# One LayerNorm group for token tiles 0 and 1, GpSimd multiplies ordered behind VectorE's, and a new list of the first tasks

## The chip, the cores and the metric

The kernel runs on one core of one Trainium2 chip. The metric is the device time of one execution in microseconds (us), the median of several runs. A core has five engines that run side by side, each through its own list of instructions in order: TensorE (PE in the profile; its weight loads, which overlap its matmuls, are PEld), VectorE (DVE), ScalarE (ACT), GpSimd (POOL), and SyncE (SP), which here issues nearly all transfers (DMAs). They wait for each other by semaphores.

## What is computed

The reference is one transformer block with a linear attention, for 2048 tokens of width 512 (32 heads of 16) and a gated feed-forward part of width 1376. A vector `c` gives six rows of modulation.

```
mod = silu(c) @ w_mod                    # sa, ca, ga, sb, cb, gb, 512 each
h   = layernorm(x) * (1 + ca) + sa
q, k, v = h @ wqkv, per head
pq, pk  = q @ w_phi, k @ w_phi           # per head, 16 x 16
phi_q   = [softmax(pq), softmax(-pq)]    # phi_k alike from pk
kv = phi_k^T v ;  z = sum of phi_k over the tokens
o  = (phi_q kv) / (phi_q z + 1e-6)
x  = x + ga * (o @ wo)
h  = layernorm(x) * (1 + cb) + sb
x  = x + gb * ((sigmoid(h @ w_gate) * (h @ w_up)) @ w_down)
```

Weights, inputs and the output are bf16.

## The kernel before

The tokens are cut into 16 tiles of 128. Everything is a task: a name, the engines that it may run on with the planner's costs, what it reads and writes, and the buffers that it uses (class `Graph`, L109). The program's order is the string `ORDER` (L39): every task's name once, in one list, with `@A`, `@D` or `@P` where it doesn't run on its first engine. `arrange` (L137) hands out the buffers in this order, `emit` (L270) issues the tasks in this order, and each engine runs its own in the order of the list. So the list is the schedule: a task that isn't ready holds up whatever stands behind it on its engine. There are eight PSUM banks, seven 2 KB buffers for features (`r2k`), eight `xn` buffers and so on (`CAPS`, L250).

The stages, by task names (the number is the token tile unless said):

- Start: `ld_...` are SP's loads (of x, wk, wv, pieces `wm` of w_mod, and so on); `warm` are matmuls on zeros that fill TensorE's time (`warm0` is six, `warm1_0` to `warm1_11` one each); `c1`, `c2`, `c3` make silu(c). `tpw`, `wTc`, `fold`, `foldc` fold w_phi into the key weights, and with `wqT` (a transposing load) into the query weights. `modc1.0` and `modc1.1` with their copies `modc1c0`, `modc1c1` make sa and ca; `modca` makes ga, `modc2` the other three rows.
- First LayerNorm (L695 to L760), in groups `LG` of tiles: `st1` the statistics (VectorE, two instructions), `rs1` the reciprocal root of a group, `nmr1` minus mean times root (one small instruction a tile), `xn1` the normalized tile, then for each of four column blocks `tph` (TensorE transposes it) and `hm1` (scale and shift into `h1T`). Two groups (`TD`) are transposed by DMA (`xT1`) instead.
- Keys and values: `K` and `V` are four matmuls of 512 columns each (in two halves `a`, `b` for the first tiles); `e` the two exponentials (ScalarE, L776), `n` the sums over features (VectorE, L780), `r` their reciprocals (VectorE or ScalarE), `phi` the products (L787, GpSimd or VectorE), `va` the copy of the values (L836), `kv` the accumulation into two banks. `kvz`, `kvn` mask the sums into `kvb` (L294, L299).
- Queries: `Q`, `qe`, `qn`, and `qphi` in two halves (L784), then `pT`, a transpose by DMA.
- From there, tile by tile: `num` (phi_q times kv), `rd`, `u` (division), `tpo`/`oT`, `out` (times wo), `x1`, the second LayerNorm (`st2`, `rs2`, `nmr2`, `xn2`, `xnT`, `mod`), and in chunks of 1, 1, 2, 4, 4 and 4 tiles the feed-forward part: `g`, `u` with a dot in its name, `tg` (tanh), `hm`, `y`, `fin`, `st`. `tsw` switches ScalarE's table to tanh. `wo` and `wd` multiply ga and gb into the weights (GpSimd, L851 and L860); gb and ga go through DRAM (`gw`, `gr`) to be spread over the partitions. `ld_wd2` loads the last piece of w_down, into the tile that the `warm` matmuls read, so it waits for the last of them.

Of the kernel before, what the change touches and what calls it, by code (L numbers as in the profile page):

```python
# [39 lines left out]
bd wdz warm0 c1 warm1_0 warm1_1 warm1_2 warm1_3 warm1_4 warm1_5 ld_x0b ld_x0a ld_wk0 tpw1 tpw0 warm1_6 warm1_7 c2 mask4 st1_3 st1_2 st1_1 ld_x1b rs1_2 rs1_1  # L40
nmr1_2 ld_wk1 xn1_3@A c3 wTc1 ld_x1a pmem tpw2 wTc0 nmr1_1 st1_6 wTc2 ld_wm00b st1_0 tpw3 xn1_1 tph13 tph10 xn1_2 tph22 tph20 tph21 wTc3 fold10 rs1_0@P fold12
st1_7 foldc10 ld_wm00a foldc12 fold11 modc1.0 rs1_4@P ld_x2b warm1_8 warm1_9 foldc11 modc1c0 st1_5 tph11 tph12 warm1_10 ld_wm01b warm1_11 st1_4 rs1_3@P
hm1_20@A xn1_0 nmr1_4 hm1_10 hm1_11@A hm1_21@A tph01 tph23 fold13 tph00 xn1_6 xn1_7 ld_wm01a st1_11 hm1_01@A foldc13 st1_10 modc1.1 K3a modc1c1@D ld_x2a
hm1_00@A tph02 nmr1_3 hm1_23 rs1_6@P hm1_13@A hm1_02 st1_9 st1_8 xn1_5 tph03 K0a tph41 hm1_03@A K2a tph40 xn1_4 hm1_22@A hm1_12@A hm1_41@A hm1_40 wqT1 nmr1_6
ld_x3a st1_15 fold01 K2b foldc01 tph42 hm1_42@A K0b K3b e0.0 ld_wv0 tph32 tph30 tph31 wqT3 tph33 rs1_5@P nmr1_5 K1a hm1_32 xn1_11 hm1_30@A st1_14 n0.0 st1_12
xn1_10 e2.0 xn1_9 K1b e3.0 rs1_8@P V3a V3b va3 V0a wqT2 xn1_8 V2a hm1_31@A V2b tph43 nmr1_8 xn1_15 xn1_14 ld_wmga wqT0 V0b fold03 V1a modca.0 modca.1 hm1_33
tph50 e1.0 n2.0 V1b K5a r0.0@A modcac hm1_50 n3.0 hm1_43@A foldc03 xT1_11 fold02 tph52 fold00 foldc02 phi0.0 va2 foldc00 xT1_10 va1 n1.0 va0 K5b K4a r3.0
# [8 lines left out]
qn6.0 wo0 wo3 kv15.0 kvz0 kvn0 kv13.4 kv14.4 kv15.4 kvz1 kvn1 num0a num1a num2a wo2 rd0a wo_all rd1a qe3.0 u0a num0b num4a num1b rd0b Q11 qe5.0 rd2a u0b u2a
rd4a num2b qn3.0 u1a rd1b tpo0 Q8 qphi6.0@P qphi6.1@P oT0 out0 num4b rd2b u1b wd0 qe11.0 u2b qphi3.1@P qphi3.0@P x1_0 rd4b st2_0 qe8.0 Q7 qe7.0 tpo1 oT1 Q10
Q9 out1 Q15 oT2 rs2_0 qn5.0 nmr2_0 xn2_0 u4a u4b x1_1 qn7.0 tsw xnT0 out2 qphi5.1@P qphi5.0@P pT6 mod02 mod00 qphi7.0@P pT3 mod03@A mod01@A qe15.0 qphi7.1@P
Q13 g0.8 x1_2 tg0.8 g0.1 st2_1 wd1 rs2_1 tg0.1 u0.8 u0.1 g0.0 num3b g0.4 hm0.1 hm0.8 pT5 qe9.0 tg0.4 g0.9 wd2 u0.4 u0.9 rd3b u3b tg0.9 g0.5 num3a hm0.4 hm0.9
# [999 lines left out]
```

## Time and profile before

| | |
|---|---|
| median of 3 runs | 203.47 us (203.35 to 204.83) |
| span of the execution profiled | 202.2 us |
| TensorE busy | 194.4 us, 96% of the span |
| VectorE busy | 160.6 us, 79% |
| ScalarE busy | 105.3 us, 52% |
| GpSimd busy | 104.2 us, 52% |
| mean granted clock of TensorE | 0.998 |
| moved by DMA | 22.92 MB |

The time of a run is taken outside of the profile; the span is from the profile's first instruction to its last. A timeline row is the start in us, the length in us, the engine, the line, the operation, the output and inputs with their sizes, and how many instructions were merged into it; in brackets the idle time before it and what ended that. A group row has count, busy time, mean ns of one, and idle time before it. Neighbouring instructions of an engine overlap a little, so the time that one costs is from its start to the next one's. Matmuls are pipelined: a matmul of 512 columns is 379 ns long in the records, while the next can start well before its end.

### The profile page before, as it was taken

What the parts mean: (1) busy time and instruction counts of PE and PEld (TensorE: products, weight loads), DVE (VectorE), ACT (ScalarE), POOL (GpSimd) and SP (SyncE); (2) the same over time, 40 slices, a digit from 0 to 9 for tenths busy, and PEclk for the clock granted to TensorE, in tenths of its full rate; (3) what the DMA queues carried; (4) which work ended last, traced back from release to release, by engine and by line L of the source; (5) the groups of instructions that cost most, each with busy time, mean ns of one, the idle gap of its engine ahead of it and who ended that gap; (6) DMA issues with size and microseconds to landing.
All of it is one profiled execution on the core that took longest, in us unless ns stands there. A gap on an engine that the chain in (4) does not pass through costs nothing.

```text
span 202.2 us, 4128 instructions
## 1 busy us (share of the span) xinstructions
PE 194.4 (96%) x1447; PEld 106.2 (53%) x1471; DVE 160.6 (79%) x376; ACT 105.3 (52%) x250; POOL 104.2 (52%) x146
## 2 busy tenths in 40 slices
PE   7989999999989999999999999999999999999993
PEld 2545656455464787668844444444444444444442
DVE  3999999999999999998897796885969753326622
ACT  2899999999978975576531215212113420334100
POOL 3889978799699998867570066130030431000000
PEclk9999999999999999999999999999999999999999
DMA  5999965669963992418664243542113031000011
GB/s 169 329 262 239 289 232 111 114 71 261 396 254 77 133 109 51 82 39 108 117 79 80 53 79 85 100 104 52 26 26 81 2 78 54 28 5 26 28 54 57
DMA packets 49452, 22.92 MB, mean 113 GB/s; under 512 B 38065, under 2 KB 47634, under 8 KB 49426
## 3 DMA queue, kind: packets, MB, share of 16 engines
q1 hardware_dynamic: 48896, 22.59, 50.1%
q8 instruction: 12, 0.20, 0.4%
q14 instruction: 14, 0.11, 0.2%
q10 hardware_dynamic: 530, 0.02, 0.2%
HBM read 11.58 MB, written 2.10 MB: 68 GB/s over the span
## 4 chain that ended last, share of the span: by engine, by line
PE 70%; ACT 15%; DVE 8%; issue 2%; POOL 2%; DMA 1%; POOLq 0%; DVEq 0%
PE y_ps L485 19%; PE u_ps L447 18%; PE g_ps L447 18%; PE a_ps L356 5%; ACT h1T L751 3%; ACT e L776 3%; ACT qe L776 2%; PE num L326 2%; PE k_ps L817 2%; DVE qks L780 2%; ACT wqk_f L685 2%; PE v_ps L821 2%; DVE ks L780 1%; DMA x_sb<-in_A_x_dram 1%; DVE phi L787 1%
## 5 line engine op out<-in xcount | busy, mean ns | idle before, releaser
L457 ACT ACTIVATE tg<-g_ps 128x512 bf16<-128x512 f32 (+5 forms) x66 | 28.7, 455 | 66.8 <-PE g_ps L447 39.9
L468 DVE SCALAR_TENSOR_TENSOR wmod_sb<-tg,u_ps 128x512 bf16<-128x512 bf16 (+4 forms) x63 | 30.2, 491 | 18.0 <-ACT tg L457 11.5
L485 PE MATMUL y_ps<-wd_sb,wmod_sb 128*128 128x512 bf16 (+4 forms) x180 | 44.2, 366 | 0.2
L447 PEld LDWEIGHTS <-wg_sb 128*128 128x128 bf16 (+1 forms) x252 | 21.9, 99 | 16.1 <-issue 0.2
L447 PEld LDWEIGHTS <-wu_sb 128*128 128x128 bf16 (+1 forms) x252 | 21.7, 99 | 15.9 <-issue 0.3
L784 POOL TENSOR_TENSOR qphi<-qe,qks 128x512 bf16<-128x512 bf16 x24 | 25.1, 1064 | 4.1 <-DMA pT<-qphi 1.4
L485 PEld LDWEIGHTS <-wmod_sb 128*128 128x128 bf16 (+1 forms) x187 | 17.1, 98 | 16.0 <-issue 0.6
L447 PE MATMUL u_ps<-wT_sb,wu_sb 128*128 128x512 bf16 (+2 forms) x124 | 23.8, 322 | 0.1
L447 PE MATMUL g_ps<-wT_sb,wg_sb 128*128 128x512 bf16 (+2 forms) x122 | 23.0, 321 | 0.2
L447 PE MATMUL g_ps<-wqk_sb,wg_sb 128*128 128x128 bf16 (+4 forms) x127 | 19.9, 287 | 0.1
L447 PE MATMUL u_ps<-wqk_sb,wu_sb 128*128 128x128 bf16 (+4 forms) x127 | 19.8, 286 | 0.2
L780 DVE TENSOR_REDUCE ks<-e 128x64 f32<-128x1024 bf16 (+2 forms) x22 | 19.3, 904 | 0.2
L492 DVE TENSOR_TENSOR ot<-y_ps,x 128x512 bf16<-128x512 f32 (+2 forms) x17 | 11.1, 654 | 10.1 <-PE y_ps L485 10.1
L780 DVE TENSOR_REDUCE qks<-qe 128x64 bf16<-128x1024 bf16 x16 | 19.1, 1204 | 0.0
L376 POOL TENSOR_SCALAR ve<-mv 128x2 f32<-128x2 f32 (+1 forms) x8 | 1.8, 226 | 33.4 <-DVE mv L366 33.3
L776 ACT ACTIVATE e<-k_ps 128x512 bf16<-128x512 f32 (+2 forms) x44 | 18.3, 536 | 0.0
L776 ACT ACTIVATE qe<-q_ps 128x512 bf16<-128x512 f32 x32 | 17.1, 612 | 0.8 <-POOL phi L787 0.6
L787 POOL TENSOR_TENSOR phi<-e,kr 128x1024 bf16<-128x1024 bf16 (+2 forms) x10 | 14.9, 1501 | 2.5 <-DVE phi L787 1.2
L817 PE MATMUL k_ps<-wqk_f,h1T 128*128 128x512 bf16 x61 | 16.1, 379 | 0.1
L356 PE MATMUL a_ps<-wo_sb,oT 128*128 128x512 bf16 x60 | 15.9, 379 | 0.2
L871 PE MATMUL q_ps<-wqk_f,h1T 128*128 128x512 bf16 x61 | 15.7, 379 | 0.2
L821 PE MATMUL v_ps<-wv_sb,h1T 128*128 128x512 bf16 x61 | 15.3, 379 | 0.1
(132 smaller groups left out, 307.7 us busy)
## 6 DMA issues: line engine op xcount, KB each, us to landing
out_dram<-ot SPq DMA_DIRECT2D x15, 128.0 KB, 1.8
x_sb<-in_A_x_dram SPq DMA_DIRECT2D x6, 256.0 KB, 5.1
wmod_sb<-in_w_mod_dram SPq DMA_DIRECT2D x1, 1536.0 KB, 7.0
wu_sb<-in_B_w_up_dram SPq DMA_DIRECT2D x1, 1376.0 KB, 10.9
wg_sb<-in_B_w_gate_dram SPq DMA_DIRECT2D x1, 1376.0 KB, 10.3
wd_sb<-in_B_w_down_dram SPq DMA_DIRECT2D x1, 1280.0 KB, 7.9
wmod_sb<-in_w_mod_dram SPq DMA_DIRECT2D x4, 256.0 KB, 6.2
wqk_sb<-in_A_wqkv_dram SPq DMA_DIRECT2D x2, 256.0 KB, 4.8
```

Source lines behind the costliest of these rows:

```text
L356: pe.matmul(ap_[:], lhsT=oT[:, j, :], rhs=wo_sb[:, j, :], start=(j == 0), stop=(j == KT - 1))
L447: pe.matmul(ps[:fsz, 0:n], lhsT=w[:, j, ft * P:ft * P + fsz], rhs=h[:, j, 0:n], start=(j == 0), stop=(j == KT - 1))
L457: G.add(f"tg{k}.{ft}", {"ACT": 0.13 + n * 0.00083}, lambda e, tg=tg, g_ps=g_ps, fsz=fsz, n=n: act.activation(tg[:fsz, 0:n], g_ps[:fsz, 0:n ...
L468: dve.scalar_tensor_tensor(hm_all[:fsz, hm[k].slot, ft, 0:n], tg[:fsz, 0:n], 1.0, u_ps[:fsz, 0:n], op0=ALU.add, op1=ALU.mult)
L485: mm = pe.matmul(y[:, 0:c1 - c0], lhsT=hm_all[:fsz, hm[k].slot, ft, tl * P:(tl + 1) * P], rhs=wd_sb[:fsz, ft, c0:c1], start=(ft == 0), sto ...
L776: act.activation(ee[:, a:b, s].rearrange("p g f h -> p g (f h)"), kp[:, a * 64:b * 64].rearrange("p (g n) -> p g n", n=64), ACT.Exp, scale ...
L780: dve.tensor_reduce(ks[:, a:b].rearrange("p g s h -> p (g s) h"), ee[:, a:b].rearrange("p g s f h -> p (g s) h f"), axis=AX.X, op=ALU.add)
L784: engine(e).tensor_tensor(ph[:].rearrange("p (g s f h) -> p g s f h", s=2, f=DH, h=4)[:, :, s], ee[:, :, s], ks[:, :, 1 - s].unsqueeze(2). ...
L787: engine(e).tensor_tensor(ph[:, a * P:b * P].rearrange("p (g f h) -> p g f h", f=DH, h=4), ee[:, a:b].rearrange("p g s f h -> p (g s) f h" ...
L817: pe.matmul(kp[:], lhsT=h1T[:, j, t * P:(t + 1) * P], rhs=wqk_f[:, j, D:2 * D], start=(j == 0), stop=(j == KT - 1))
L821: pe.matmul(vp[:], lhsT=h1T[:, j, t * P:(t + 1) * P], rhs=wv_sb[:, j, :], start=(j == 0), stop=(j == KT - 1))
L871: pe.matmul(qp[:], lhsT=h1T[:, j, t * P:(t + 1) * P], rhs=wqk_f[:, j, 0:D], start=(j == 0), stop=(j == KT - 1))
```

## The change

Three things change.

The first LayerNorm's groups: tiles 0 and 1, which were groups of one, are one group; `rs1_0` now serves both, `tph0.j` transposes both tiles, `hm1_0.j` scales both. The tasks are named after the first tile of the group now (`hm1_2.1` was `hm1_21`, `hm1_10.0` was `hm1_60`). `xn1_0`, which ran on VectorE, takes the form of the others (GpSimd or ScalarE, with `nmr1_0`).

`emit` keeps the last instruction of the last VectorE task that counts as a user of the port (`phi`, `qphi`, `xn1`, `xn2`, `wo`, `wd`, some `hm1` and `mod`), and each later GpSimd task except `rs` gets a dependence on it, that is, waits for it, whether or not it uses its data.

`ORDER` is a new list as a whole. Of the rest that the diff adds (`HALF`, `QHALF`, `ROWS`, `WPQ`, `RPAIR`), all is switched off.

```diff
-LG = [[0], [1], [2, 3], [4, 5], [6, 7], [8, 9], [10, 11], [12, 13], [14, 15]]
-TD = [0, 0, 0, 0, 0, 0, 1, 1, 0]
+LG = [[0, 1], [2, 3], [4, 5], [6, 7], [8, 9], [10, 11], [12, 13], [14, 15]]
+TD = [0, 0, 0, 0, 0, 1, 1, 0]
...
+XP = list(range(16))
+PIN = 1
...
     def emit(order):
+        pinned = None
         for t in order:
...
+            body = nc.cur_bb.bb.instructions
+            n0 = len(body)
             t.fn(t.eng)
+            if PIN and t.eng in t.port and not t.name.startswith("rs"):
+                if t.eng == "DVE":
+                    pinned = body[-1].name
+                elif pinned:
+                    tc.add_manual_dep(body[n0], pinned, mybir.DependencyInfo(mybir.DependencyClass.Sync, mybir.DependencyReason.DATA), reason="port order")
```

The head of the new list, with TensorE's first keys and the first exponential:

```
bd wdz c1 warm0 pmem mask4 ld_x0a st1_1 st1_0 rs1_0 ld_x0b st1_2 nmr1_0 xn1_0 xn1_1@A c2 st1_3 rs1_2 ld_x1b st1_6 st1_7 rs1_6@P ld_wk0 tpw0 tpw1 wTc0 warm1_0
warm1_1 wTc1 ld_wk1 tpw2 tpw3 wTc3 wTc2 fold10 foldc10 fold13 foldc13 fold12 foldc12 tph0.0 fold11 foldc11 c3 nmr1_2 xn1_2 xn1_3 ld_x1a st1_5 nmr1_6 st1_4 rs1_4
ld_x2a st1_8 ld_wm00b ld_wm00a warm1_2 tph0.1 modc1.0 modc1c0@D hm1_0.0@A tph2.2 tph2.1 tph0.3 warm1_3 hm1_2.1@A tph2.3 tph2.0 xn1_7 xn1_6 warm1_4 warm1_5
warm1_6 hm1_2.0@A hm1_0.1@A ld_x2b st1_10 nmr1_4 xn1_4 xn1_5 st1_9 rs1_8@P st1_11 ld_wm01a ld_wm01b modc1.1 modc1c1 hm1_2.2 tph6.0 hm1_6.0@A tph0.2 hm1_0.2@A
hm1_0.3@A K3a K0a tph4.2 hm1_4.2@A tph4.0 K1a tph4.1 hm1_4.1@A K0b e0.0 hm1_2.3 K3b e3.0 tph6.2 tph6.3 K1b K2a e1.0 ...
```

Further on: `V4 e4.0 rs1_14 tph8.0 kv0.0 Q1 qe1.0 tph8.2 Q0 qe0.0 V3a V3b K5a va3 phi1.0@D kv1.0`; `warm1_7` stands ahead of `kv3.0`, `warm1_8` and `warm1_9` about `kv10.0`; at the end of the sums `kv15.0 kvz0 kv15.4 kvz1 kvn0 kvn1 qe7.0 Q5 qe5.0 wo0 wo1 wo_all num0a`, then `num4a Q8 warm1_10 warm1_11 ld_wd2 grb u0b tpo0 oT0`, and `xnT0 mod02@A mod01@A mod00@A mod03@A out4 Q10 ... st2_1 rs2_1 g0.2 tsw g0.9 tg0.9`. Before, that last place read `xn2_0 ... tsw xnT0 out2 ... mod02 mod00 ... mod03@A mod01@A`, and Q7 stood behind the sums.

More of the change, by code (lines that the diff above doesn't have):

```diff
@@ L39 @@
 ORDER = """
[L40 to L47, printed above, removed]
@@ L56 @@
[L56 to L59, printed above, removed]
@@ new lines @@
+nmr1_8 xn1_9 st1_13 rs1_12@P n0.0 hm1_6.2 hm1_6.3 hm1_4.0 ld_wv0 V0a wqT3 V2a wqT2 V0b tph4.3 hm1_4.3@A K2b e2.0 V2b tph6.1 va2 va0 wqT0 wqT1 fold01 fold02 V1a
+V1b va1 fold00 foldc00 xn1_8 tph8.3 xn1_11 nmr1_12 xn1_12 r0.0 phi0.0 n3.0 r3.0@A phi3.0 ld_wmga xT1_10 ld_wo xT1_11 hm1_10.3@P xn1_13 K4a K4b fold03 foldc03
+n1.0 hm1_8.3 foldc01@D hm1_6.1 st1_14 modca.0 modca.1 modcac r1.0@A foldc02 n2.0 V4 e4.0 rs1_14 tph8.0 kv0.0 Q1 qe1.0 tph8.2 Q0 qe0.0 V3a V3b K5a va3 phi1.0@D
+kv1.0 hm1_8.2@A hm1_8.0@A r2.0 nmr1_14 xn1_15 hm1_10.2@P phi2.0@D kv2.0 Q2 qe2.0 V5 tph8.1 hm1_8.1@A xn1_14@A warm1_7 kv3.0 K5b e5.0 qn1.0 qphi1.0@P qn0.0
@@ new lines @@
+phi8.0@D K15 va8 kv8.0 V14 va9 kv9.0 K12 r10.0 phi10.0 e14.0 n14.0 e13.4 n13.4 r14.0 phi14.0 r13.4 phi13.4 e13.0 n13.0 e14.4 va10 n14.4 r13.0 phi13.0 warm1_8
+kv10.0 Q6 kv11.0 warm1_9 kv11.4 kv11.2 kv11.6 e15.0 n15.0 r15.0 phi15.0 e15.4 n15.4 e12.0 n12.0 r14.4@A phi14.4@D qe6.0 r15.4@A phi15.4@D gra wo3 wo2 ld_wg0
+ld_wu0 ld_wd gwb r12.0@A phi12.0@D qn6.0 V13 va13 Q3 qe3.0 qn3.0 qphi3.0@P V12 Q7 V15 va12 kv12.0 kv13.0 kv13.4 qphi3.1 pT3 va14 kv14.4 va15 kv14.0 kv15.0 kvz0
+kv15.4 kvz1 kvn0 kvn1 qe7.0 Q5 qe5.0 wo0 wo1 wo_all num0a rd0a num1a rd1a u0a num0b rd0b num1b num4b rd4b num4a Q8 warm1_10 warm1_11 ld_wd2 grb u0b tpo0 oT0 u1a
@@ new lines @@
+u4b rd1b rd4a u1b qphi6.0@P qphi6.1@P pT6 qn5.0 qphi5.0@P u4a oT4 qphi5.1@P pT5 qe8.0 Q9 qe9.0 out0 x1_0 tpo1 oT1 num2b rd2b Q11 qe11.0 st2_0 rs2_0 wd7 qn7.0
+qphi7.1@P qphi7.0@P wd3 Q15 qe15.0 nmr2_0 num2a rd2a Q13 num3a rd3a num3b u2b u3a u2a oT2 out1 x1_1 rd3b num6a rd6a num6b rd6b u3b oT3 xn2_0 xnT0 mod02@A
+mod01@A mod00@A mod03@A out4 Q10 u6a x1_4 u6b oT6 wd0 pT7 st2_1 rs2_1 g0.2 tsw g0.9 tg0.9 u0.9 tg0.2 u0.2 hm0.2 hm0.9 out2 qe10.0 num5b rd5b g0.7 tg0.7 g0.0
+tg0.0 x1_2 qe13.0 nmr2_1 xn2_1 g0.8 num5a rd5a u0.10 u5b u0.0 hm0.0 u5a oT5 u0.7 hm0.7 qn11.0 out3 tg0.8 g0.10 tg0.10 hm0.10 g0.1 xnT1 mod12@A mod10@A mod11@A
@@ L234, with f_wp @@
     act.dma_start(c_row[:], c)
-    with nc.allow_non_contiguous_dma(reason="small w_phi load"):
-        act.dma_start(wp_sb[:], A_w_phi.rearrange("(kt hl) d f -> (hl d) kt f", hl=8))
+    def f_wp(e):
+        with nc.allow_non_contiguous_dma(reason="small w_phi load"):
+            e.dma_start(wp_sb[:], A_w_phi.rearrange("(kt hl) d f -> (hl d) kt f", hl=8))
+    if not WPQ:
+        f_wp(act)
     act.preload_act_table_set("natural_log_exp_and_others")
@@ L539, in load_wm @@
     def load_wm(i):
+        if ROWS:
+            load(f"wm0{i}", [("wmod0", i, 0), ("wmod0", i, 1)], lambda e: sp.dma_start(wmod_sb[:, 2 * i:2 * i + 2, 0:2 * D], wmod_v[:, 2 * i:2 * i + 2, 0:2 * D]), 512 * K1)
+            return
         for s in range(2):
@@ L645, in f_mc2 @@
         act.add(modc[:, 12:16], ps[:, 4:8], 1.0)
-    for h in range(2):
-        modc1_task(h)
+    if ROWS:
+        modc1_rows()
+    else:
+        for h in range(2):
+            modc1_task(h)
     modc_task("modca", list(range(8, 12)), ["wmod_ga", "wmod_ga"], ["gcola"], lambda ps: act.copy(gcol[:, 0:4], ps[:]), 0.2)
```

125 lines of the change are left out of this document (75 added, 50 removed).

## The prediction

> **What bounds the kernel now.** I read the page's first part, then the busy time by stretch, the timeline by engine, and the groups by form.
>
> ```profile
> PE 194.4 (96%) x1447; PEld 106.2 (53%) x1471; DVE 160.6 (79%) x376; ACT 105.3 (52%) x250; POOL 104.2 (52%) x146
> ```
>
> ```profile
> 6.50:13.60 7.10, 6.10 (x85) 4.06 (x85) 6.61 (x21) 6.75 (x16) 5.95 (x15) 1.00 1.20 277
> 13.60:57.40 43.80, 42.80 (x399) 23.90 (x403) 43.28 (x91) 42.69 (x116) 38.05 (x43) 1.00 0.90 226
> 57.40:80.00 22.60, 22.30 (x257) 15.47 (x261) 21.66 (x66) 17.65 (x44) 22.36 (x23) 1.00 0.61 102
> 80.00:199.00 119.00, 117.98 (x702) 61.07 (x714) 85.75 (x191) 35.92 (x71) 34.53 (x52) 1.00 0.31 61
> ```
>
> The columns are length, then busy PE, PEld, DVE, ACT, POOL. From 13.6 us (the first key projection) to 199 us TensorE sits idle for 1.0 + 0.3 + 1.0 = 2.3 us in all. Until 57.4 us VectorE (43.28 of 43.80) and ScalarE (42.69) are as full as TensorE: three engines set that stage together. After it TensorE alone does. The work of TensorE is the same in both orders, so the end moves only by the time in which TensorE does nothing of use. Where that time lies:
>
> ```profile
> 10.93 0.81 PE L600 MATMUL warm<-wd_sb 128*128 128x512 bf16 x2
> ...
> 13.62 0.38 PE L817 MATMUL k_ps<-wqk_f,h1T 128*128 128x512 bf16 x1
> ...
> 14.93 0.59 PE L817 MATMUL k_ps<-wqk_f,h1T 128*128 128x512 bf16 x2
> ...
> 57.38 0.93 PE L326 MATMUL num<-kvb,pT 128*128 128x68 bf16 x24 [0.43 <-DVE kvb L294]
> ```
>
> Fillers (warm) run at a pitch of about 0.43 us (0.81 less the 0.38 of a lone matmul), and the keys of 14.93 at 0.59 - 0.38 = 0.21 us: the array worked at half rate until about 14 us. At 57.38 it waits for the masked key-value sums (kvb). So a gain has at most those 2.3 us and what an earlier start of the keys brings.
>
> **The start.** The first piece of x is asked for at the same time, so VectorE's statistics begin as before at 3.66. On ScalarE the new list up to the first key scaling pair (hm1_2.0, after which K3a can start) is rs1_0, xn1_1, c2, rs1_2, four wTc, four foldc, rs1_4, three hm1.
>
> ```profile
> 5.46 0.29 ACT L709 ACTIVATE ve<-mv,eps 128x2 f32<-128x2 f32 x1 [1.08 <-DVE mv L703]
> 5.79 0.20 ACT L710 ACTIVATE rs<-ve 128x2 f32<-128x2 f32 x1
> ...
> 6.63 0.80 ACT L727 ACTIVATE xn<-x_sb,nmr,rs 128x512 bf16<-128x512 bf16 x1
> 7.33 2.14 ACT L664 COPY wT_sb<-tp_w 128x512 bf16<-128x512 bf16 x4
> 9.43 1.56 ACT L685 CAST wqk_f<-fold_ps 128x512 bf16<-128x512 f32 x3
> ...
> 17.06 1.14 ACT L776 ACTIVATE e<-k_ps 128x512 bf16<-128x512 f32 x2
> ...
> 20.84 0.71 ACT L751 ACTIVATE h1T<-tp_h,modc 128x256 bf16<-128x256 bf16 x1
> 21.30 1.22 ACT L776 ACTIVATE e<-k_ps 128x512 bf16<-128x512 f32 x2
> ```
>
> Back to back, a task costs its start-to-start time: xn 0.70 (6.63 to 7.33), wTc 0.52 (2.10 / 4), foldc 0.48, rs 0.5, an exponential pair about 0.95 (1.14 without its tail of some 0.2), an hm1 of two tiles 0.46 (20.84 to 21.30). From 6.63: 0.70 + 0.15 + 0.5 + 2.1 + 1.9 + 0.5 + 3 x 0.46 = 7.2, so K3a starts at 13.85, against 13.62. Up to e0.0 another 0.25 (modc1c1) and six hm1 (2.8): 16.8, against 17.06. Merging tiles 0 and 1 replaces six single scalings on ScalarE and two on VectorE by four double ones on ScalarE; the gain is spent on the added hm1_4.1, hm1_4.2 and hm1_6.0 ahead of e0.0. One more piece of x stands ahead of w_mod in SP's queue.
>
> ```profile
> 10.51 0.47 PEld L630 LDWEIGHTS <-wmod_sb 128*128 128x128 bf16 x16 [0.79 <-DMA wmod_sb<-in_w_mod_dram]
> ```
>
> 256 KB at the 277 GB/s of the stretch are 0.95 us: modc1.0 would start near 11.4 instead of 10.5, and VectorE reaches its copy only at 12.1, ScalarE the first scaling at 12.45: hidden, by a few tenths. I cost the start at 0, with ends -0.5 and +0.5.
>
> **VectorE up to the key-value sums.** Counted in the two orders up to kvn1, the new one has more: qn 1, r 3, qphi 2, foldc 1, nmr 1 instruction; fewer: phi of 1024 columns 2, phi of 256 columns 3, r of 16 columns 1, xn1_0, single hm1 2.
>
> ```profile
> L780 DVE TENSOR_REDUCE qks<-qe 128x64 bf16<-128x1024 bf16 x5 | 5.9, 1211 | 0.0
> L787 DVE TENSOR_TENSOR phi<-e,kr 128x1024 bf16<-128x1024 bf16 x7 | 4.5, 673 | 0.0
> ...
> L718 DVE TENSOR_SCALAR nmr<-mv,rs 128x1 f32<-128x1 f32 x15 | 2.4, 200 | 0.0
> L798 DVE RECIPROCAL kr<-ks 128x64 bf16<-128x64 f32 x4 | 2.2, 538 | 0.0
> ...
> L784 DVE TENSOR_TENSOR qphi<-qe,qks 128x512 bf16<-128x512 bf16 x3 | 1.2, 420 | 0.0
> L294 DVE TENSOR_TENSOR kvb<-kvacc,mask 128x256 bf16<-128x256 f32 x2 | 0.8, 410 | 0.0
> L787 DVE TENSOR_TENSOR phi<-e,kr 128x256 bf16<-128x256 bf16 x3 | 0.8, 295 | 0.0
> ...
> L798 DVE RECIPROCAL kr<-ks 128x16 bf16<-128x16 f32 x4 | 0.7, 204 | 0.0
> L753 DVE TENSOR_SCALAR h1T<-tp_h,modc 128x128 bf16<-128x128 bf16 x2 | 0.7, 336 | 0.0
> ...
> L729 DVE TENSOR_SCALAR xn<-x_sb,mv,rs 128x512 bf16<-128x512 bf16 x1 | 0.4, 382 | 0.0
> ```
>
> Neighbours overlap by some 0.08 us, which I take off each mean. More: 1.13 + 3 x 0.46 + 2 x 0.34 + foldc + 0.12. A fold copy on VectorE is not in the trace: half its width from PSUM took 410 ns (0.33 net), so 0.33 to 0.66; I take 0.55, nearer the double. Sum 3.86. Less: 2 x 0.59 + 3 x 0.21 + 0.12 + 0.30 + 2 x 0.26 = 2.75. Net **+1.1 us** on an engine without a gap, so the masked sums come 1.1 later, near 58.7. ScalarE's own count to there rises by about 1.3 (one qe 0.95; rs1_0, rs1_4 and rs1_14 come to it while one goes, xn1_14 comes, single scalings and three r go): the same size, so it doesn't hide VectorE's.
>
> TensorE has one query projection more done by then, 4 x 0.216 = 0.86, and Q5 now stands between the last kv and num0a, which covers the wait of 0.43. Net cost at the first num: 1.1 - 0.86 + 0.1 for the sums that now come in pairs (kvz0, kvz1, kvn0): **+0.35** (ends -0.4, if VectorE's list loses some of its early stalls, and +1.1).
>
> **TensorE's lead.** Before, K4 is ready far ahead of its exponential:
>
> ```profile
> 24.80 0.59 PE L817 MATMUL k_ps<-wqk_f,h1T 128*128 128x512 bf16 x2
> ...
> 32.07 1.19 ACT L776 ACTIVATE e<-k_ps 128x512 bf16<-128x512 f32 x2
> ```
>
> almost 7 us. In the new order Q1, Q0, K5, Q2, V6, K6 follow each other so that ScalarE reaches each exponential within about half a microsecond of its projection, and V4 and kv0.0 (phi0 now behind three xn on GpSimd) stand ahead of Q1, which needs foldc02, ScalarE's task at 25.0. Nothing is queued behind TensorE that could cover it. Five fillers stand behind K3a, each 0.22 us in TensorE's queue. [...] I take **+0.4**; the ends are 0 and 1.5, half of some 3 us at half rate (before, from 10.93 to about 14).
>
> **The pins.** PIN makes a GpSimd task wait for VectorE's last multiply or scaling that stands ahead in the order. Behind such a wait stand GpSimd's next tasks and, through pT, SP's queue. Nearly all pinned pairs (phi6.0 on phi5.0, qphi6.0 on qphi3.1) lie far apart in the order. What could be won:
>
> ```profile
> 20.02 0.71 POOL L713 TENSOR_TENSOR rs<-ve,mhalf 128x2 f32<-128x2 f32 x1
> ...
> 26.89 1.15 POOL L713 TENSOR_TENSOR rs<-ve,mhalf 128x2 f32<-128x2 f32 x1
> ...
> 48.44 0.62 POOL L787 TENSOR_TENSOR phi<-e,kr 128x256 bf16<-128x256 bf16 x1
> 48.87 0.33 DVE L787 TENSOR_TENSOR phi<-e,kr 128x256 bf16<-128x256 bf16 x1
> ```
>
> A VectorE multiply that began inside GpSimd's took 0.33 against a mean of 0.295; GpSimd's rs beside three VectorE multiplies took 1.15 against 0.71. Only GpSimd lost, and it has slack (38.05 of 43.80). So 0, with ends -0.2 and +0.3. [...]
>
> **After the sums.** The table switch (tsw) now follows four modulations on ScalarE, no longer precedes two.
>
> ```profile
> 64.71 0.81 ACT L400 ACTIVATE xn<-x,nmr,rs 128x512 bf16<-128x512 f32 x1 [0.40 <-DVE nmr L383]
> 65.55 1.28 ACT L387 ACT_TABLE_LOAD   x1
> 66.84 0.81 ACT L426 ACTIVATE wqk_sb<-tp_x,modc 128x128 bf16<-128x128 bf16 x2
> ```
>
> From xn2_0 to the first tg: 0.72 + 0.35 (transposes) + 4 x 0.35 + 1.28 = 3.75, against 3.79 before, where a qe lies between. TensorE has out2, g0.7, g0.0 and g0.8 to go on with; **+0.2**, ends 0 and 1.28 (the whole load bare). The last piece of w_down (ld_wd2) waits for warm1_11 and grb follows it, so wd7 and behind it qphi7 and pT7 may wait on GpSimd; num7 stands some 9 us further on: 0, ends 0 and 1.
>
> Sum against the execution profiled: 202.2 + 0.35 + 0.4 + 0.2 = 203.15, or +0.95. The span of 202.2 has 1.3 us less than the median of 203.47; the same offset gives **204.4 us**.
>
> **The rivals.** (a) *Covered, no loss*: VectorE's extra reduction is fully paid back by the query that is done earlier, and the wait of 0.43 at 57.38 goes with some 0.3 of the other idle time before 80 us: 203.47 - 0.7 = 202.8. For it: Q5 ahead of num0a. Against: VectorE has no gap to give back. A gain of over 2 us would take nearly all idle time after 13.6. (b) *Half-rate keys* (slower): place K3a to K2a; price 1.5 us of TensorE instead of 0.4, and with no lead some 0.5 at the hand-overs to ScalarE: 204.4 + 1.1 + 0.5 = 206.0. It decides if the keys still run at a pitch of 0.43 at 15.5 us. [...] (c) *The late last piece*: gb lands after 66, GpSimd stands at wd7 and num7 waits 1 to 2 us: 205.9. (d) *Multiplies block each other*: a VectorE multiply is held behind GpSimd's phi, whose wide form takes
>
> ```profile
> L787 POOL TENSOR_TENSOR phi<-e,kr 128x1024 bf16<-128x1024 bf16 x5 | 9.8, 1958 | 0.6 <-PE kvacc L282 0.3 <-ACT vaug L836 0.2
> ```
>
> 1.96 us: phi5.0, on VectorE soon after phi4.0 on GpSimd, would cost up to that: 206.3. The pins then do nothing, since they only hold GpSimd back. Against it stands the stretch of 0.04 above. [...]
>
> **How the numbers follow.** Forecast 0.50 (204.4; its own range 203.6 to 205.3), (a) 0.22, (b) 0.15, (c) 0.08, (d) 0.05. A measurement of this kernel tells about 1%, 2.03 us, from no change: below 201.4 or above 205.5. Faster takes the far end of (a): 0.08. Slower is (b), (c), (d) in most of their cases and a little of the forecast's tail: 0.27. The rest, 0.65, is within 1%. The low end, 202.6, is 203.47 with -0.4 at the sums and -0.5 at the start; the high end, 206.7, takes +1.1, +1.5 and about half of 1.28 in place of mine.
>
> **What would show it.** Right: the first num near 58.5 to 59; VectorE without idle to there; TensorE idle of some tenths in 14 to 26; GpSimd waits of under 1 us that name VectorE's multiplies. Wrong: a num before 57.5, TensorE idle of over 2 us between 14 and 57, or a new wait on wd or pT7 between 64 and 77.

## The result: slower by 2.5%, and the profile after

The changed kernel takes **208.74 us** (median; 208.21 to 209.01) against 203.41 for the kernel before, a ratio of 1.0249 with a 95% interval of 1.0228 to 1.0271. My forecast was 204.4 with a range up to 206.7, and "within 1%" as the likeliest: the time lies above the range. The profiled execution has a span of 206.8 us against 202.2. Ratios in this document leave out an execution that the record marks as slow; among the variants below that is one each of e1, e7, e11 and e12.

The lines that answer to those shown of before, in the same order. First the page's first part, then the busy time by stretch, cut at the first key projection and the first num of this kernel (14.75 and 61.28 us; before 13.62 and 57.38). The columns are length, then busy PE, PEld, DVE, ACT, POOL, then the granted clock.

```profile
PE 194.6 (94%) x1446; PEld 106.9 (52%) x1471; DVE 162.3 (78%) x373; ACT 106.2 (51%) x251; POOL 103.6 (50%) x141
```

```profile
6.50:14.75 8.25, 7.34 (x88) 5.56 (x90) 7.79 (x28) 7.31 (x19) 6.25 (x13) 1.00 1.14 327
14.75:61.28 46.53, 44.32 (x397) 24.20 (x402) 45.68 (x84) 44.64 (x119) 41.17 (x43) 1.00 0.87 201
61.28:84.00 22.72, 22.28 (x260) 15.59 (x265) 21.01 (x67) 17.01 (x44) 19.53 (x21) 1.00 0.58 99
84.00:203.60 119.60, 117.50 (x695) 60.67 (x706) 84.01 (x186) 35.27 (x69) 33.28 (x50) 1.00 0.29 58
```

The stretch up to the first num grew from 43.80 to 46.53 us, and VectorE is still full in it (45.68). TensorE's idle time, 2.3 us before, is now 2.2 + 0.4 + 2.1 = 4.7 us. Two waits stand out on the timeline of TensorE, the second with the row of VectorE that ends it:

```profile
61.28 0.93 PE L344 MATMUL num<-kvb,pT 128*128 128x68 bf16 x24 [0.93 <-DVE kvb L312]
...
171.36 0.14 DVE L543 TENSOR_SCALAR flag<-bs 1x1 int32<-1x1 f32 x1
...
172.24 2.11 PE L503 MATMUL y_ps<-wd_sb,wmod_sb 96*128 96x512 bf16 x8 [1.30 <-DVE flag L543]
```

The first num waits longer for the masked sums (0.93, before 0.43) and comes at 61.28, not near 58.7. And a wait that the kernel before doesn't have: at 172.24 TensorE waits for the flag.

To see where the time went I take, for some tasks, the start less the time of all real products that stand ahead in TensorE's list (a 128x512 product at its pitch of 0.216 us, the median from one start to the next in the traces of before and after; smaller ones in proportion, an estimate). What is left is idle time, fillers and slow running:

| task | before: start, left | after: start, left | grown by |
|---|---|---|---|
| Q1 | 26.43, 10.72 | 25.20, 11.19 | 0.47 |
| kv10.0 | 51.54, 10.92 | 51.65, 12.76 | 1.84 |
| num0a | 57.38, 11.81 | 61.28, 14.84 | 3.03 |
| tpo0 | 59.14, 11.83 | 63.34, 15.29 | 3.46 |
| out6 | 76.68, 12.22 | 77.61, 15.92 | 3.70 |
| y10.0 | 161.56, 12.54 | 165.15, 16.13 | 3.59 |
| y9.10 | 169.35, 12.69 | 174.40, 17.74 | 5.05 |

So 3.0 us are lost by the first num, 0.4 at the two fillers behind Q8, 0.2 up to out6, and 1.5 at the flag; some 0.4 come back behind the last product. (The column "left" depends a little on what the small products are put at; the growth hardly does.)

The 3.0 us have two parents that run side by side. **VectorE** reaches its last masked sum at 61.06 instead of 57.24, 3.8 us late. By the mean durations of before its list has grown by 1.04 us. Of the other 2.8 us some 2.5 are in multiplies that last longer than before. The timeline, each with the multiply of GpSimd beside it:

```profile
33.93 1.05 POOL L832 TENSOR_TENSOR qphi<-qe,qks 128x512 bf16<-128x512 bf16 x1
34.02 1.24 DVE L832 TENSOR_TENSOR qphi<-qe,qks 128x512 bf16<-128x512 bf16 x1
...
54.70 1.05 POOL L835 TENSOR_TENSOR phi<-e,kr 128x512 bf16<-128x512 bf16 x1
55.05 0.98 DVE L835 TENSOR_TENSOR phi<-e,kr 128x512 bf16<-128x512 bf16 x1
...
59.30 1.05 POOL L832 TENSOR_TENSOR qphi<-qe,qks 128x512 bf16<-128x512 bf16 x1 [0.19 <-DVE qks L828]
59.32 1.31 DVE L832 TENSOR_TENSOR qphi<-qe,qks 128x512 bf16<-128x512 bf16 x1
```

A qphi that took 0.42 before takes 1.24 (qphi2.0) and 1.31 us (qphi3.1), and each ends 0.28 after GpSimd's: 33.93 + 1.05 = 34.98 against 35.26, and 60.35 against 60.63. The middle pair is phi14.4 beside phi15.0, 56.03 against 55.75. Over their usual lengths these three have 0.83 + 0.55 + 0.90 = 2.3 us. VectorE is *held* while GpSimd multiplies.

**ScalarE** starts its last copy of values, va15, at 58.39 instead of 55.43, 3.0 us late: from 5.4 us on its busy time has grown by 1.2 us (48.88 to 50.07) and its idle time by 1.9 (1.09 to 2.96). The three largest waits that the kernel before does not have, with the row of TensorE behind the first:

```profile
6.72 1.03 PE L701 MATMUL tp_w<-ident,wqk_sb 128*128 128x128 bf16 x8 [1.67 <-DMA wqk_sb<-in_A_wqkv_dram]
7.55 1.06 PE L623 MATMUL warm<-wd_sb 128*128 128x512 bf16 x2
8.40 1.06 PE L701 MATMUL tp_w<-ident,wqk_sb 128*128 128x128 bf16 x8
...
9.50 0.59 ACT L704 COPY wT_sb<-tp_w 128x512 bf16<-128x512 bf16 x1 [0.88 <-PE tp_w L701]
...
39.78 1.43 ACT L819 ACTIVATE e<-k_ps 128x512 bf16<-128x512 f32 x4 [0.66 <-DVE qphi L832]
...
51.63 2.19 ACT L819 ACTIVATE e<-k_ps 128x256 bf16<-128x256 f32 x6 [0.39 <-POOL phi L835]
```

The last two are waits for a buffer: e7.0 gets the one that qphi4.0 sets free, e15.0 the one of phi10.0. Both engines are late by about the same; TensorE has one query projection (0.86) more behind it, which leaves the 3.0 and 2.1 us of the two.

### The profile page after: what moved, and what is told of

It is laid out like the page before. It is cut to its first block, busy times and chain, and to the rows that moved or that the text cites. A ratio compares the mean times of both kernels' runs of the same rounds, so it can differ in the third digit from the quotient of the medians.

```text
span 206.8 us, 4138 instructions
## 1 busy us (share of the span) xinstructions
PE 194.6 (94%) x1446; PEld 106.9 (52%) x1471; DVE 162.3 (78%) x373; ACT 106.2 (51%) x251; POOL 103.6 (50%) x141
## 4 chain that ended last, share of the span: by engine, by line
PE 73%; DVE 9%; ACT 5%; DMA 4%; POOL 3%; issue 3%; SPq 1%; DVEq 0%; ACTq 0%
PE y_ps L503 18%; PE u_ps L465 17%; PE g_ps L465 17%; PE a_ps L374 5%; DVE ks L828 4%; PE q_ps L921 3%; POOL phi L835 3%; PE v_ps L871 3%; DVE qks L828 2%; PE k_ps L867 2%; DMA wqk_sb<-in_A_wqkv_dram 2%; DMA oT<-o 2%; PE num L344 2%; PE g_ps L467 1%; PE warm L623 1%
## 5 line engine op out<-in xcount | busy, mean ns | idle before, releaser
L832 POOL TENSOR_TENSOR qphi<-qe,qks 128x512 bf16<-128x512 bf16 x21 | 22.2, 1068 | 3.4 <-DVE qks L828 1.7
L835 POOL TENSOR_TENSOR phi<-e,kr 128x1024 bf16<-128x1024 bf16 (+2 forms) x15 | 20.2, 1365 | 1.1 <-DVE phi L835 0.8
L871 PE MATMUL v_ps<-wv_sb,h1T 128*128 128x512 bf16 x61 | 15.9, 379 | 0.2
```

The lines of the kernel that those rows point to most:

```text
L832: engine(e).tensor_tensor(ph[:].rearrange("p (g s f h) -> p g s f h", s=2, f=DH, h=4)[:, :, s], ee[:, :, s], ks[:, :, 1 - s].unsqueeze(2). ...
L835: engine(e).tensor_tensor(ph[:, a * P:b * P].rearrange("p (g f h) -> p g f h", f=DH, h=4), ee[:, a:b].rearrange("p g s f h -> p (g s) f h" ...
L871: pe.matmul(vp[:], lhsT=h1T[:, j, t * P:(t + 1) * P], rhs=wv_sb[:, j, :], start=(j == 0), stop=(j == KT - 1))
```

## The experiments

The theory after the result: (1) a VectorE multiply that begins just after GpSimd's is held to its end, and these holds are most of what I missed; (2) the pins cost time too, since GpSimd waits; (3) the flag's load stands too early; (4) the five late fillers (ahead of kv3.0, kv10.0 and kv11.4, and two ahead of tpo0) cost TensorE their time. The rivals are that the holds or the fillers are covered by other waits, that the pins help, and that the merged group itself is slower. Times are medians; ratios are against the kernel before.

**Pins off in the changed kernel (e1), and pins on in the old list (e4).** The first sets one constant:

```diff
-PIN = 1
+PIN = 0
```

> The changed kernel with the pins off (PIN = 0), all else the same. If the new list costs and not the pins (VectorE multiplies caught behind a GpSimd multiply at 34.0, 55.1 and 59.3 us, fillers, the early flag): 207.5 to 209.5, since the pins only hold GpSimd back and these three collisions are there without them. If the pins cost: near 205, 3 us or more faster than 208.7.

The second puts the pinning part of the diff's emit into the kernel before and leaves its list.

> The kernel before (old groups, old list) with the pins added. If pins are harmless where the list has slack: 203.2 to 203.9. If waits that they add on GpSimd reach the path: 204.5 to 206.

Without pins the new list takes 210.73 us (ratio 1.0345, 1.0316 to 1.0375), 2.0 more than with them, which neither of the two cases expected. The timeline shows why:

```profile
55.25 3.81 DVE L835 TENSOR_TENSOR phi<-e,kr 128x512 bf16<-128x512 bf16 x3
...
55.87 2.65 POOL L901 TENSOR_TENSOR wo_sb<-wo_sb,ga_sb 128x512 bf16<-128x512 bf16 x2
```

phi14.4, phi15.4 and phi12.0 take 3.81 us together instead of 1.92 (55.05 to 56.97 in the changed kernel): wo3 and wo2 now run when phi15.4 and phi12.0 come, and hold both. With the pins on in the old list it is 210.01 us (1.0321, 1.0294 to 1.0348), 6.6 slower. The timeline by engine:

```profile
33.44 1.89 PE L829 MATMUL v_ps<-wv_sb,h1T 128*128 128x512 bf16 x8
...
37.58 2.24 POOL L792 TENSOR_TENSOR qphi<-qe,qks 128x512 bf16<-128x512 bf16 x2 [4.99 <-DVE phi L795]
...
39.85 1.08 ACT L784 ACTIVATE e<-k_ps 128x512 bf16<-128x512 f32 x2 [2.87 <-POOL qphi L792]
...
40.97 1.22 DVE L788 TENSOR_REDUCE ks<-e 128x64 f32<-128x1024 bf16 x1 [2.43 <-ACT e L784]
40.99 2.78 PE L829 MATMUL v_ps<-wv_sb,h1T 128*128 128x512 bf16 x8 [2.68 <-ACT e L784]
```

qphi1.1 stands right behind phi4.0 in that list, so its pin makes GpSimd idle for 5 us; qphi1.0 behind it keeps the buffer that e6.0 needs, ScalarE stands for 2.87, VectorE for 2.43 and TensorE for 2.68. Part of the 6.6 us comes behind that: the granted clock is 0.50 from 41.9 to 45.2 us (0.992 over the whole execution, 0.998 in that of the kernel before), and eight products take 2.78 us in place of 1.89. So a pin is no free thing: in the old list the pins cost 6.6 us with what they bring about, in the new one, which was written with them, they save 2.0.

**The flag's load behind st8 (e2).**

```diff
-st10 y8.9 bndd ldf mod80@P y8.10
+st10 y8.9 bndd mod80@P y8.10
...
-st8 tg5.2 hm5.7
+st8 ldf tg5.2 hm5.7
```

> The changed kernel with one task moved: ldf, TensorE's load of the flag, stands after st8 again as in the old list, no longer right behind bndd. If TensorE's wait of 1.3 us on the flag at 172.2 is a loss that nothing later covers: 1.3 to 1.6 us faster, 207.2. If the last stage has that slack anyway: 208.7.

207.56 us (1.0222, 1.0189 to 1.0256): the median is 1.2 lower than that of the changed kernel, though the two intervals overlap; the span of the profiled execution is 1.7 lower (205.1). What is sure is the wait, which TensorE's row at that place no longer has:

```profile
168.78 4.49 PE L503 MATMUL y_ps<-wd_sb,wmod_sb 128*128 128x512 bf16 x19
```

**The grouping alone (e7).** The list of before with the tiles 0 and 1 in one group (rs1_0 behind st1_0 and st1_1, tph0.j and hm1_0.j of two tiles at the places of tile 0's, tile 1's own left out), no pins.

> The kernel before with the grouping alone: tiles 0 and 1 in one LayerNorm group (rs, two-tile transposes and scalings at the places where those of tile 0 stood, the single ones of tile 1 left out), the rest of the old list and no pins. If the grouping itself is to blame for the slower start (it was costed at nothing): K0a late, 204 to 205. If the order and the pins are to blame and the grouping is harmless: 202.8 to 203.8 against 203.4.

204.11 us (1.0016, 0.9997 to 1.0036): no difference. The merged group is not the cause. (xn1_0 stays on VectorE here; in the changed kernel it is on GpSimd.)

**The fillers early (e6).** Five fillers from behind K3a go ahead of tpw0 (the names count up along the list):

```diff
-rs1_6@P ld_wk0 tpw0 tpw1
+rs1_6@P ld_wk0 warm1_0 warm1_1 warm1_2 warm1_3 warm1_4 tpw0 tpw1
```

> The changed kernel with its five late fillers (ahead of kv3.0, kv10.0, kv11.4, and two ahead of tpo0) put ahead of tpw0, where TensorE waits some 2.1 us for wk. Theory (each costs TensorE its 0.22 us, because it has no slack): 207.6 to 208.0 in place of 208.7, with the first num 0.3 to 0.7 earlier. Rival (they stand where TensorE would have waited for VectorE's list all the same): first num within 0.2 of 61.28, the two ahead of tpo0 cost something at most, 208.2 to 208.8.

208.58 us (1.0244, 1.0194 to 1.0295): no gain at the end. But the trace says more than the time. Its timeline of TensorE, at the start and at 75 us, and the one row of the changed kernel that answers to the last:

```profile
6.58 0.62 PE L701 MATMUL tp_w<-ident,wqk_sb 128*128 128x128 bf16 x8
7.04 0.59 PE L623 MATMUL warm<-wd_sb 128*128 128x512 bf16 x2
7.47 0.61 PE L701 MATMUL tp_w<-ident,wqk_sb 128*128 128x128 bf16 x8
...
75.65 1.04 PE L374 MATMUL a_ps<-wo_sb,oT 128*128 128x512 bf16 x3 [1.03 <-DMA oT<-o]
```

```profile
75.62 1.04 PE L374 MATMUL a_ps<-wo_sb,oT 128*128 128x512 bf16 x3
```

With the gap ahead of wk filled, the transposes of wk take 0.62 in place of 1.03 us, ScalarE's wait of 0.88 is gone, the first num comes 0.45 and tpo0 0.88 earlier. Then out3 starts at the same instant as in the changed kernel: it waits for the transposed oT3, which landed 4.9 us after its issue. What the start had won ended there.

The gap alone doesn't settle the rate, though. All five traces with the fillers early (e6, e8, e10, e13, e14) have transposes of 0.61 to 0.62 us, and six of the seven with the fillers late 1.03 to 1.04; but the seventh, e12, has the changed kernel's list up there and the same gap, and yet:

```profile
6.73 0.62 PE L701 MATMUL tp_w<-ident,wqk_sb 128*128 128x128 bf16 x8 [1.68 <-DMA wqk_sb<-in_A_wqkv_dram]
```

**The pairs put apart (e3, e5, e9, e12).** Four tries to take the holds away by turning the pairs. All put qphi2.0 ahead of qphi2.1. They differ in the other two:

```diff
 e3: phi15.0 wo3 wo2 behind phi12.0; qphi3.1 ahead of qphi3.0
 e5: r14.4 phi14.4 phi15.0 ahead of n12.0; qphi3.1 ahead of qphi3.0
 e9: r14.4 phi14.4 ahead of n12.0; wo3 wo2 behind phi12.0; qphi3.1 ahead of qphi3.0
 e12: as e9, but qphi3.0 behind qphi3.1 at the latter's old place
```

> The changed kernel with three pairs turned round, nothing added: qphi2.0 (VectorE) ahead of qphi2.1 (GpSimd), qphi3.1 ahead of qphi3.0, and phi15.0, wo3, wo2 (GpSimd) behind phi14.4, phi15.4 and phi12.0 (VectorE), so that the pins hold GpSimd until VectorE's multiply is through. [...] If the long multiplies are only an effect of how the profile times them, or VectorE isn't what sets the first num: 208.7, first num still near 61.3.

> The changed kernel, with the three pairs of multiplies that meet put apart and nothing moved between engines: qphi2.0 (VectorE) ahead of qphi2.1 (GpSimd), phi14.4 (VectorE) ahead of n12.0 and of GpSimd's phi15.0, qphi3.1 (VectorE) ahead of GpSimd's qphi3.0. Theory (a VectorE multiply that begins just after a GpSimd multiply is held to its end): qphi2.0, phi14.4 and qphi3.1 take 0.4 to 0.5 us each in place of 1.24, 0.98 and 1.31, the first num comes 1.0 to 2.2 us earlier than 61.28, and the kernel takes 206.5 to 207.8 in place of 208.7. Rival (the lengths come from VectorE's own memory traffic, whoever is beside it, or the stretches are covered by other waits): the multiplies stay near 1 us or the first num stays within 0.4 us of 61.28; 208.3 to 209.1.

Both failed, the other way round: 211.0 (1.0381, 1.0351 to 1.0411) and 212.03 us (1.0417, 1.0361 to 1.0473). The timeline of e5 by engine:

```profile
54.58 1.08 ACT L819 ACTIVATE e<-k_ps 128x512 bf16<-128x512 f32 x2 [1.81 <-POOL phi L835]
...
56.08 0.43 DVE L835 TENSOR_TENSOR phi<-e,kr 128x512 bf16<-128x512 bf16 x1 [2.14 <-ACT kr L843]
...
56.67 1.05 POOL L835 TENSOR_TENSOR phi<-e,kr 128x512 bf16<-128x512 bf16 x1 [2.12 <-DVE phi L835]
```

phi14.4 takes 0.43 now, so the hold is gone, but e12.0 ahead of it waits for GpSimd. The list hands the seven large buffers on first come, first served (Graph.arrange); with phi15.0 moved, e12.0 gets the buffer that phi13.0 sets free at 54.5 and not the one that kv10.0 left long ago. e3 has the same wait, of 1.81 us. In e5's trace TensorE also stands 2.11 us ahead of kv12.0 until 60.20, and behind that its granted clock is 0.50 from 61.7 to 65.0 us (0.992 over the execution); e3's trace has the same wait, of 2.23 us, and no such fall (1.000 over the execution).

> The changed kernel with the three pairs put apart once more, this time with GpSimd's phi15.0 left at its place (so that e12.0 doesn't wait for a buffer): qphi2.0 ahead of qphi2.1, r14.4 and phi14.4 ahead of n12.0, wo3 and wo2 behind phi12.0, qphi3.1 ahead of qphi3.0. Theory (a VectorE multiply that begins just after GpSimd's is held to its end, and these holds are most of what came over my count on VectorE): the three multiplies take 0.4 to 0.6 us each (qphi3.1 perhaps 0.8, if wo2 still runs), the first num comes at 59.3 to 60.3 in place of 61.28, and the kernel takes 207.0 to 207.9. Rival (the holds are covered by waits for other things): the first num stays within 0.4 us of 61.28, 208.3 to 209.1.

208.75 us (1.0263, 1.0232 to 1.0294). qphi2.0 takes 0.49 in it, qphi3.1 0.42 and phi14.4 0.68, so the holds are gone but for 0.25, and yet (the timeline, TensorE's rows behind VectorE's):

```profile
33.08 0.49 DVE L832 TENSOR_TENSOR qphi<-qe,qks 128x512 bf16<-128x512 bf16 x1
...
59.32 0.42 DVE L832 TENSOR_TENSOR qphi<-qe,qks 128x512 bf16<-128x512 bf16 x1
...
58.22 1.39 PE L300 MATMUL kvacc<-vaug,phi 128*128 128x68 bf16 x32 [0.92 <-ACT vaug L886]
60.39 0.93 PE L344 MATMUL num<-kvb,pT 128*128 128x68 bf16 x24
62.11 1.02 PE L921 MATMUL q_ps<-wqk_f,h1T 128*128 128x512 bf16 x3 [0.79 <-ACT qe L819]
...
60.97 2.06 ACT L819 ACTIVATE qe<-q_ps 128x512 bf16<-128x512 f32 x4 [1.83 <-POOL qphi L832]
```

The num comes at 60.39, 0.89 earlier, not 2: now TensorE waits 0.92 for ScalarE's va, whose start hasn't moved (va15 at 58.51, in the changed kernel 58.39). Behind it the gain is lost to one more change of buffers: qe7.0 gets qphi3.0's.

> The changed kernel with the three pairs put apart and every buffer passed on in the same rotation as there (qphi3.0 moved behind qphi3.1 in place of qphi3.1 ahead, so that qe7.0 takes the buffer that kv12.0 frees, and not the one that qphi3.0 frees). Theory A (the holds cost VectorE 2.1 us, and what was won at the first num in the last try was lost to qe7.0's wait for a buffer alone): first num at 60.2 to 60.6, no wait of TensorE for ScalarE's qe behind it, and the kernel at 207.6 to 208.1 in place of 208.7. Theory B (the holds are covered twice, VectorE's next tasks have other waits, and TensorE is bound right behind the sums by GpSimd's and ScalarE's lists as well): first num near 60.4, tpo0 as late as before (63.3 to 63.6), 208.4 to 209.

Three executions took 207.35 to 208.77 us (median 208.08; 1.0233, 1.0181 to 1.0284), the fourth 210.82. The median of the three lies in theory A's range, but they reach into the changed kernel's 208.21 to 209.01, so the time decides nothing. In the trace qe7.0 no longer waits for GpSimd, the first num comes at 60.71, a little past theory A's 60.2 to 60.6, and tpo0 at 62.76, 0.58 earlier than in the changed kernel, where theory B has it as late as before; out6 keeps 0.51 of that. Between kv3.0 and the first num TensorE loses 2.54 us instead of 3.42. In this execution another pair met, though. The first key projection comes 0.7 us earlier in it (14.04, with wk's transposes at full rate), but behind this pair that is gone: kv3.0 comes at 31.21, in the changed kernel at 30.91. The pair:

```profile
26.31 0.78 POOL L772 TENSOR_SCALAR xn<-x_sb,rs,nmr 128x512 bf16<-128x512 bf16 x1
26.31 1.32 DVE L835 TENSOR_TENSOR phi<-e,kr 128x1024 bf16<-128x1024 bf16 x1
```

The same pair in the changed kernel, where GpSimd was the one to wait:

```profile
26.61 1.27 POOL L772 TENSOR_SCALAR xn<-x_sb,rs,nmr 128x512 bf16<-128x512 bf16 x1
...
26.62 0.70 DVE L835 TENSOR_TENSOR phi<-e,kr 128x1024 bf16<-128x1024 bf16 x1
```

**The repairs together (e8, e10, e13, e14).** e8 is e5, e2 and e6 in one; e10 is e9, e2 and e6 with out3 moved behind g0.5; e13 is e12, e2 and e6; e14 is e13 with out2 behind g0.8 and x1_2 behind u5b.

> The changed kernel with the three repairs together: the three pairs put apart, the load of the flag moved behind st8, the five fillers early. If the three losses are separate and add up: 204.0 to 205.5, so that what is left against the kernel before (some 1 to 2 us) is the new order of the first stage. If they cover one another: 206 to 207.5.

> The changed kernel with all of it: the pairs put apart as in the run before, the flag's load behind st8, the five fillers ahead of tpw0, and out3 four steps later (behind g0.5), because with the fillers early TensorE waited 1.2 us there for the transposed oT3. If the losses add up (some 1.3 for the pairs, 1.3 for the flag, 0.5 to 0.9 for fillers and out3): 205.0 to 206.0, and what is left against the kernel before is VectorE's longer list. If they cover one another: 206.5 to 207.5.

> The changed kernel with the pairs put apart in that way, the flag's load behind st8 and the five fillers ahead of tpw0; out3 left at its place. Theory A: the gains add up to some 2.7 to 3.2 us, less 0.3 to 0.9 that out3's wait for the transposed oT3 may take back: 205.8 to 206.8. Theory B: as the repairs so far, 207.0 to 207.5.

> The run before (pairs put apart with the buffers' rotation kept, flag late, fillers early) with out2 three steps later on TensorE (behind g0.8) and its x1_2 behind u5b on VectorE, because there TensorE stood 1.85 us for the transposed oT2. Theory A (the gain of 1.7 us that stood at tpo0 was lost to that wait alone, so that the losses found add up when nothing behind them takes them back): 205.2 to 206.2. Theory B (the stretch of 66 to 80 us has a bound of its own, in the transfers of SyncE's queue, and another wait there takes the place of this one): 206.6 to 207.6.

e8 took 209.3 us (1.0305, 1.0226 to 1.0384), with e5's order of phi15.0 and its wait of 1.81 us for a buffer in it; e10 207.26 (1.0176, 1.0151 to 1.02), the best median and the only interval that lies below the changed kernel's; e13 207.9 (1.0231, 1.0171 to 1.0291); e14 207.79 (1.0235, 1.0178 to 1.0293), its four runs from 206.47 to 209.18. TensorE in e13, then in e14:

```profile
61.68 0.40 PE L363 MATMUL tpo<-ident,o 128*128 128x128 bf16 x4
...
73.48 1.04 PE L374 MATMUL a_ps<-wo_sb,oT 128*128 128x512 bf16 x4 [1.69 <-DMA oT<-o]
```

```profile
61.43 0.40 PE L363 MATMUL tpo<-ident,o 128*128 128x128 bf16 x4
...
73.28 1.04 PE L374 MATMUL a_ps<-wo_sb,oT 128*128 128x512 bf16 x4 [0.61 <-DMA oT<-o]
```

tpo0 comes 1.66 and 1.91 us earlier than the 63.34 of the changed kernel, and out2 gives most of it back to the transposed oT2: out6, behind it, starts at 77.94 and 76.94, in the changed kernel at 77.61. e14 fits theory B better than A, for the wait at out2 only became shorter and the median is no lower; but 207.79 lies above the ranges of both, and that the transposing transfers bound the stretch from 66 to 80 us is read from e6, e13 and e14, not tested. What is won ahead of 70 us isn't always lost there: of what stood at tpo0, e6 and e13 keep nothing at out6, e14 keeps 0.67 of 1.91, e12 0.51 of 0.58. The 206.47 us of e14's profiled execution are the least of all runs with repairs; its other three took 207.2 to 209.18.

**The old kernel's own wait (e11).** Q11 ahead of num0a in the list of before.

> The kernel before with the query projection Q11 moved ahead of num0a, into the 0.43 us in which TensorE waits for the masked sums; nothing else. If that wait is bare time of TensorE: 202.8 to 203.1 against 203.4. If the later tpo0 and out0 give it back (VectorE's o is ready when Q11 used to end, 0.86 us of TensorE's work now missing there): 203.3 to 203.8.

203.71 us (1.0006, 0.9994 to 1.0018): the wait for the sums is gone, but TensorE waits as much behind it for VectorE's o. No version here is faster than the kernel before.

## Why the prediction was wrong, point by point

**The pins: this step failed.** I wrote "A VectorE multiply that began inside GpSimd's took 0.33 against a mean of 0.295" (the stretch of 0.04 in rival (d)) and "Only GpSimd lost", and so put nothing for VectorE's waits; in the changed kernel three held multiplies alone cost VectorE 2.3 us. The row was read wrongly. GpSimd's multiply ran from 48.44 to 49.06, VectorE's from 48.87 to 49.20: it ended 0.14 after GpSimd's. The nine held multiplies in the traces of before and after all do so, at a distance that goes with their size: 0.14 us for 256 columns (this one), 0.28 for 512 (seven, among them the three above), 0.55 for 1024 (phi8.0: 47.66 to 48.56, GpSimd's to 48.01). The usual 0.295, 0.42 and 0.67 less these leave 0.15, 0.14 and 0.12. My estimate from these three differences is a fixed part that can pass while GpSimd still runs, and a part by size that comes after; the multiply at 48.87 began so late that hardly more than its fixed part lay inside GpSimd's time. I compared durations where I should have compared ends.

In the rows above whose starts lie apart (by 0.09 us at 34.02, by 0.35 at 55.05, by 0.43 at 48.87) GpSimd began first and VectorE waited. With VectorE ahead, by 0.16 us at 56.28 in the changed kernel, it was GpSimd: wo3, at 56.44, took 1.55 us, the three after it (wo2, wo0, wo1) 1.16 to 1.17. Where the starts lie closer the record doesn't tell which of the two waits: at 26.61 GpSimd is recorded 0.01 us ahead and yet took 1.27 instead of 0.78, and at 26.31 in e12, recorded together, VectorE waited (1.32 instead of 0.67). What makes the one wait for the other no run shows.

The same step had the price of the pins at 0 and, in rival (d), that "the pins then do nothing". Both fell: e1 shows 2.0 us saved, because a pinned GpSimd multiply can't begin ahead of the VectorE multiply it would hold (the three of e1's row take 3.81 us without pins, 1.92 with them); e4 shows 6.6 us lost where the pinned pair stands close together, others need GpSimd's buffers, and TensorE's clock is lower behind its wait (0.50 from 41.9 to 45.2). Rival (d) had the right cause and the right sign (206.3), at a chance of 0.05; but phi5.0, which I named, was not held; qphi2.0, phi14.4 and qphi3.1 were.

**VectorE's count was right.** I said +1.1, the mean durations along both lists give +1.04, and the fold copy that I put at 0.55 took 0.68 with its tail. ScalarE's count, +1.3 by my reckoning, came to +1.2. What both lacked were the waits: 2.8 us more on VectorE (2.3 of them the three holds), 1.9 on ScalarE (wk's transposes and two buffers above all). "Net +0.35 at the first num" and "+0.4 for the lead", 0.75 together, became 3.0. e9 shows how the two stand: with nearly all of the three holds gone the num comes 0.9 earlier, not 2.3, for now TensorE waits for ScalarE's copies of the values, which are as late as they were (3.0, less the 0.86 of the added query: 2.1). As far as e9 goes, the holds are bare for 0.9 us and covered by ScalarE for the rest; that VectorE alone sets the sums was half of it. And e9 isn't faster at the end: its 0.9 us go to qe7.0's buffer.

**The start.** K3a came at 14.75, past my range's end (13.85 + 0.5). I had counted ScalarE's list and left TensorE's rate out: the transposes of wk ran at half rate (1.03 against 0.62), and ScalarE waited 0.88 for them. The 1.67 us without work ahead of them are not the whole reason, as e12 shows; what decides the rate there stays open. Rival (b) had a half rate but put it at the keys; they ran at full rate (four at 14.75 in 1.03 us, a pitch of 0.65 / 3 = 0.22). And the half rate "until about 14 us" in the old kernel I had misread from four fillers. Rows of the same trace, before and among them, are at full rate:

```profile
7.20 0.59 PE L600 MATMUL warm<-wd_sb 128*128 128x512 bf16 x2
7.96 0.62 PE L661 MATMUL tp_w<-ident,wqk_sb 128*128 128x128 bf16 x8 [0.16 <-DMA wqk_sb<-in_A_wqkv_dram]
...
11.79 0.27 PE L744 MATMUL tp_h<-ident,xn 128*128 128x128 bf16 x2
```

Two fillers at 7.20 stand 0.59 - 0.38 = 0.21 us apart, and a transpose of 0.22 us at 11.79 costs 0.05. Why the fillers at 10.93 and 11.90 stand 0.43 apart no run shows. So "half of some 3 us at half rate", the end of the range for the lead, had no ground: no run shows a half rate that lasts into the keys, and what was lost up to Q1 is 0.47 us (table above). In e6 the transposes run at full rate and the first num comes 0.45 earlier. The grouping itself is neutral, as I costed it (e7).

**After the sums.** +0.2 for the switch of tables and its neighbours came out as 0.24 from tpo0 to out6, but by luck: no product of TensorE waits at the switch (ScalarE loads the table from 71.89 to 73.18), and what was lost stands at xnT0 and at out3 (some 0.3 and 0.4 us by the reckoning of the table, where the old kernel loses about 0.5 in the same stretch). No product waits for w_down's last piece: rival (c) didn't come. The fillers cost 0.4 at tpo0. But I didn't see how late the transposed oT2 and oT3 come: in e6 and e13 the whole gain ahead of 70 us ended there, so that a gain as in (a) might not have been carried to the end.

**The late part of the list I didn't look at.** TensorE's load of the flag ran 11.8 us behind its producer in the old kernel (168.15 to 179.99) and stands right behind it in the new list. TensorE, with no slack, stood 1.46 us for it (1.30 of them as a wait in the row); e2 takes the wait away. Nothing in my sum stood for it.

Put right, the sum reads: 0.95 of the forecast, 2.3 more at the first num, 0.4 at the fillers and 1.5 at the flag: 5.1 us, against 5.05 in the table at y9.10 and 5.3 between the medians. That is a reading of the traces. The repairs take away 1.5 of the 5.3 us at best (e10); the other 3.7 no experiment gives back. What stays open above all is ScalarE's part: that its two buffer waits and its longer list hold the num at 60.4 when the holds are gone is read from the trace and not taken away by an experiment. Nor is the spread of e12 to e14 settled; that chance decides which of two multiplies comes first, as in the pair at 26.31 and 26.61, or at what rate wk's transposes run, could explain it, but each run has one trace only.

## What to carry to other kernels

Where VectorE and GpSimd both multiply, compare the ends of overlapping instructions, not their lengths: here a held one ended 0.14, 0.28 or 0.55 us after the other, by its columns, whatever its own length was (0.44 to 1.31 us at 512). In a list written by hand, a task that is moved takes other waits with it: every later task may get another buffer, and each load or flag stands at a new distance from its producer, so diff the whole list, up to its end. And when two engines are late by nearly the same at one join, repairing one of them wins only the difference.
